# Attention beside a gated MLP: x written in twelve pieces, a second half that begins with the heads at hand, and PSUM banks in a fixed round

## The chip, the cores and the metric

The kernel runs on one core of a Trainium2 chip. The core's engines work side by side, each on its own queue of instructions in the order in which they are written: TensorE (PE, matmuls into the eight banks of PSUM), VectorE (DVE), ScalarE (ACT), GpSimd (POOL) and SyncE (SP), which issues nearly all DMAs here. The metric is the device time of one execution in microseconds (us), the median of several runs.

## The reference

```python
def _A_ref(x, k_cache, v_cache, wq, wo):        # 32 heads of 128, last W = 512 keys
    q = split_heads(x @ wq)
    k, v = k_cache[:, :, Sk - W:, :], v_cache[:, :, Sk - W:, :]
    scores = jnp.einsum("bhqd,bhkd->bhqk", q, k) * (Dh ** -0.5)
    p = _softmax(scores, axis=-1)
    o = jnp.einsum("bhqk,bhkd->bhqd", p, v)
    return merge_heads(o) @ wo

def _B_ref(x, w_in, w_sp, b_sp, w_out):          # F = 1376, Fh = 688
    z = _gelu(x @ w_in)
    z1, z2 = z[..., :Fh], _layernorm(z[..., Fh:], axis=-1)
    g = jnp.einsum("ts,bsf->btf", w_sp, z2) + b_sp[None, :, None]
    return (z1 * g) @ w_out

xn = _layernorm(x)                               # x is 2048 x 512, fp32
return x + _A_ref(xn, ...) * _silu(_B_ref(xn, ...))
```

(`split_heads` and `merge_heads` stand for the reshapes and transposes of the original.)

## The kernel before

All matrices are fp32. Each operand is split into a high part, cast to fp32r (`*_h`), and the rest (`*_l`), and a product is three matmuls: high by high, high by low, low by high (`mm3`, L65 to L67). ACT casts the high part, POOL or DVE subtracts to get the rest (`rest`, L59).

The attention makes up the first 1460 us. Its 2048 query rows are taken in two halves of 1024 (w = 0 and w = 1), each half for all 32 heads, and each head has two blocks of 512 rows per half: 128 blocks `b` in all, four steps of 128 rows each, 512 steps `t`, some 2.5 us per step while nothing waits. A head's weights (keys `("h", h), 1`, values `2`, output weights `3`) are loaded piece by piece into `raw` (256 KB, L102), cast (L141) and kept in `wt`; `plan` sets the step of the split and, six steps earlier, that of the load. The counter h runs to 64, and h modulo 32 is the head. Both halves take the heads in the order 0 to 31.

One step of the main loop issues, on PE in this order: the score of step t (`score`, into a bank `ps`), some products of the projection for later blocks (`q_products`, L447), the product of the shares with the values for step t - 13 (`pv`), and the out-product of step t - 18 (`outp`, into a bank `ps`). DVE takes the score's maximum (`nm`, L474), ACT the exponential (`prob`, L476, it reads `ps`), DVE adds the out-product to the sum (`sacc`, L533, it reads `ps`) and transposes the shares of the step before in blocks of 32 (L485, into `pL`). To finish the transposition, the four steps of a block are written together to memory (`p_dram<-pL`, 1 MB, L489) and come back in six loads (`pL<-p_dram`, L497, two steps later), ACT casts them at step t + 11 (`pT_h`, L504), POOL makes the rest (`pT_l`, L59), and `pv` reads both two steps after. What is put into the list `late` is issued on DVE at the end of the step; what is in `ends` is issued after that.

SP's queue holds all these transfers in the order of the steps: the raw loads at the start of a step, stores and loads of the shares at its end, and then what `ends` has. An SP DMA also waits until the eighth before it has landed. x, normalised and transposed, is held in the blocks `X[w]`. In the first half X[0] is written to memory for the end of the kernel (`keep_x`, four writes of 1 MB: one at step -2, three at steps 22, 25 and 28), and the rows of the second half are prepared (`later_x`: eight times four transposing matmuls, `flip`, L199, then row operations in `late`: L301, or `row_sums`, L234 to L236), and written to memory. X[1] is fetched back in 28 pieces (`fetch_part`, L263) at steps 232 to 246.

Of the eight PSUM banks four belong to `ps_acc` (projection and shares by values, `ps_a`), four to `ps_step`, one pool of four buffers of one name from which score, out-product, flip and some other products draw: it gives the bank that was released first.

```python
    ps_step = psum.enter_context(tc.tile_pool(name="ps_step", bufs=4, space=PSUM))
        ps = ps_step.tile([P, W], F32, name="ps_3")
```

After step 512 come the rest of the MLP's products, the spatial product and the output projection, which the change doesn't touch.

Of the kernel before, what the change touches and what calls it, by code (L numbers as in the profile page):

```python
# [8 lines left out]
F32 = mybir.dt.float32  # L9
# [31 lines left out]
def mixer_kernel(ctx: ExitStack, tc: tile.TileContext, x, wh, w_in, w_sp, b_sp, w_out, out):  # L41
# [8 lines left out]
    nc = tc.nc  # L50
# [7 lines left out]
    def rest(engine, lo, whole, hi):  # L58
        engine.tensor_tensor(lo, whole, hi.bitcast(F32), op=OP.subtract)  # L59
# [3 lines left out]
    def mm3(ps, first, last, lhs, rhs):  # L63
        (lh, ll), (rh, rl) = lhs, rhs
        nc.tensor.matmul(ps, lh, rh, start=first, stop=False)  # L65
        nc.tensor.matmul(ps, lh, rl, start=False, stop=False)  # L66
        nc.tensor.matmul(ps, ll, rh, start=False, stop=last)  # L67

    def cols(pair, lo, hi):
        return tuple(t[:, lo:hi] for t in pair)  # L70
# [10 lines left out]
    rawp = left.enter_context(tc.tile_pool(name="rawp", bufs=4))  # L81
    psum = ExitStack()
    ps_acc = psum.enter_context(tc.tile_pool(name="ps_acc", bufs=4, space=PSUM))
    ps_step = psum.enter_context(tc.tile_pool(name="ps_step", bufs=4, space=PSUM))
    att = ExitStack()
    sp = att.enter_context(tc.tile_pool(name="sp", bufs=1))
    ap = att.enter_context(tc.tile_pool(name="ap", bufs=2))
# [8 lines left out]

    raw, wt = {}, {}

    def load_piece(key, k):
        n = NB if key[0] == "w" else 512  # L100
        r = raw[key, k] = (xq.tile([P, 512], F32, name="rawx") if key[0] == "w" else rawp.tile([P, 512], F32, name="raw"))
        nc.sync.dma_start(r[:, :n], (w_in if key[0] == "w" else wh)[key[1] % H, :, k])  # L102

    def load_early(n, cs):
        if (n, "raw") not in raw:
# [44 lines left out]
    X = {0: {}, 1: {}}  # L150

    def block():
        return x8([P, 2, 2, 512])

    def quarter(t, j):
        return t[:, :, j * P:(j + 1) * P]
# [37 lines left out]
                nc.vector.tensor_scalar(sl, sl, mean, r, op0=OP.subtract, op1=OP.mult)  # L194

    def flip(t):
        ps = ps_step.tile([P, NC, P], F32, name="ps_3")
        for c in range(NC):
            nc.tensor.transpose(ps[:, c, :], t[:, c * P:(c + 1) * P], ident)  # L199
        return ps  # L200

    def ln_flip(i, parts=1):
        n, j = divmod(i, 4)
        if j == 0:
            for h in range(2):
                X[0][h, n] = block()
        if parts == 1:
            ps = flip(sacc[:, i, :])
        else:
            ps = ps_step.tile([P, NC, P], F32, name="ps_3")  # L210
        rests, rest_of = [], []
        for h in range(2):
            if parts > 1:
                for c in (2 * h, 2 * h + 1):
                    nc.tensor.transpose(ps[:, c, :], sacc[:, i, c * P:(c + 1) * P], ident)
            hi, lo = (quarter(X[0][h, n][:, a], j) for a in range(2))
            nc.scalar.copy(hi, ps[:, 2 * h:2 * h + 2])
            rests.append((lo, ps[:, 2 * h:2 * h + 2], hi))
        if n == 1:
            p2, y = ps.rearrange("p c q -> p (c q)"), sacc[:, i, :]  # L220
            nc.scalar.copy(y[:, :256], p2[:, :256])
            rest_of.append((y[:, 256:], p2[:, 256:], y[:, :256]))
# [20 lines left out]
    def t_split(p):  # L243
        y, o = sacc[:, 4 + p, :], sacc[:, p, :]
        for name, src in (("T2", o[:, 256:]), ("T1", o[:, :256]), ("T3", y[:, 256:]), ("T4", y[:, :256])):
# [4 lines left out]
    xd = {(w, k): dram.tile([P, 2, 2, 512], F32, name=f"x_dram{w}{n}")  # L250
          for w in range(2) for n, k in enumerate([(0, 0), (1, 0), (0, 1), (1, 1)] + list(TS) * w)}

    def keep_x(k):
        nc.sync.dma_start(xd[0, k], X[0][k].bitcast(F32))

    def fetch_x(w, k):
        X[w][k] = block()
# [77 lines left out]
    def zmm(ps, i, n, cs):  # L335
        for c in cs:
            mm3(ps, c == 0, c == NC - 1, tuple(x_op(i, a, c) for a in range(2)), cols(wt[("w", n), c], 0, NB))
# [8 lines left out]
                             start=k == 0, stop=k == len(order) - 1)  # L346

    def z1_product(i, n, between=lambda: None):
        ps = ps_acc.tile([P, 512], F32, name="ps_a") if n else ps_step.tile([P, 512], F32, name="ps_3")
        zmm(ps[:, :NB], i, n, range(2))  # L350
        between()
        zmm(ps[:, :NB], i, n, range(2, NC))
        return ps
# [49 lines left out]

    def load_q(g):
        r = wraw[g] = wq.tile([P, 2, 512], F32, name="wq", bufs=2)
        h = 2 * g % H
        for k in range(2):
            nc.sync.dma_start(r[:, k], wh[h + k, :, 0])

    def q_parts(g):  # L410
        r = wraw[g]
# [54 lines left out]

    def score(t):
        b, j = divmod(t, 4)
        ps = ps_step.tile([P, W], F32, name="ps_3")
        mm3(ps, True, True, cols(qT[b], j * P, (j + 1) * P), wt[("h", where(b)[0]), 1])  # L470
        if j == 0:
            sums[b] = ap.tile([P, 4], F32, name="sums", bufs=8)
        nm = ap.tile([P, 1], F32, name="nm", bufs=8)
        nc.vector.tensor_reduce(nm, ps, axis=AX.X, op=OP.max, negate=True)  # L474
        prob[t] = ap.tile([P, W], F32, name="prob", bufs=3)
        nc.scalar.activation(prob[t], ps, AF.Exp, bias=nm, accum_out=sums[b][:, j:j + 1])  # L476
# [46 lines left out]
    def outp(b, j):  # L523
        h, qb = where(b)
        i = qb * 4 + j
        at = sacc[:, i % T8, :]
        ps = ps_step.tile([P, D], F32, name="ps_3")
        mm3(ps, True, True, cols(oT[b], j * P, (j + 1) * P), wt[("h", h), 3])
        rs = sums[b][:, j:j + 1]
        if h % H == 0:  # L530
            nc.vector.tensor_scalar(at, ps, rs, None, op0=OP.mult)
        else:
            nc.vector.scalar_tensor_tensor(at, ps, rs, at, op0=OP.mult, op1=OP.add)  # L533
        if h % H == H - 1:
            nc.sync.dma_start(s_dram[:, i, :], at)
# [6 lines left out]
    def at(t, f, *args):  # L542
        todo.setdefault(t, []).append((f, args))
# [6 lines left out]

    for h in range(2 * H):
        for k, d in ((1, -4 if h else -5), (2, 6), (3, 11)):
            if h:
                plan(("h", h), k, 8 * h + d)
            elif k > 1:
                plan(("h", 0), k, d)
# [29 lines left out]
        at(-3 + p, t_sums, p)  # L586
        at(-2 + p, t_split, p)
    ends = {}
    for t, k in ((-2, (0, 1)), (22, (0, 0)), (25, (1, 0)), (28, (1, 1))):
        ends.setdefault(t, []).append((keep_x, k))  # L590
    for k, d in enumerate((4, 6, 8, 11, 13, 15, 17)):
        for n in range(4):
            ends.setdefault(16 * (NG // 2 - 1) - LEAD + d + (0, 0, 1, 1)[n], []).append((fetch_part, 1, ORDER[k], n))
# [26 lines left out]
    power = const.tile([P, 12], F32, name="power")  # L620
    nc.vector.memset(power, -0.5)

    warm = ps_step.tile([P, NC, P], F32, name="ps_3")
    for k in range(21):
        nc.tensor.transpose(warm[:, k % NC, :], ident, ident)
    bsp = const.tile([P, NT], F32, name="bsp")
# [13 lines left out]
        rest(nc.vector, *r)  # L640
    split_piece(w0, 2, nc.vector, True)
    split_piece(w0, 3, nc.vector, True)
    ps = ps_step.tile([P, 512], F32, name="ps_3")
    zmm_in(FIRST, ps[:, :NB], 0, 0)
    ln_flip(1)
    z1_out(0, 0, ps)
# [3 lines left out]
    for k in range(2, 4):  # L650
        split_piece(w1, k, nc.vector, True)
    ln_open(3)
    ps = ps_step.tile([P, 512], F32, name="ps_3")
    zmm_in(PAIRED, ps[:, :NB], 1, 0)
    z1_out(1, 0, ps)
    ln_apply(rows[2], 2)
# [1 line left out]
    ps = ps_acc.tile([P, 512], F32, name="ps_a")  # L658
# [18 lines left out]
    for t in range(T0, T1):  # L677
# [16 lines left out]
        if 0 <= t < NSTEP:  # L694
            score(t)
# [6 lines left out]
        g, s = divmod(t + LEAD, 16)  # L702
# [6 lines left out]
        if t in DRAIN:  # L709
            ps = z1_product(*DRAIN[t])  # L710
# [19 lines left out]
    ps = z1_product(*LAST[-1])  # L730
# [276 lines left out]
```

## Time and profile before

| | before |
|---|---|
| median of 3 runs (us) | 1825.79 (1825.51 to 1826.38) |
| the profiled execution (us) | 1828.83 |
| its span (us) | 1827.1 |
| PE busy (us, share) | 1799.5 (98%) |
| DVE, ACT, POOL busy | 76%, 64%, 68% |
| PE's longest waits in the attention | for ACT's pT_h 8.1 us (2 times), for DVE's sacc 4.3 us (7), for POOL's pT_l 4.1 us (8) |

A row of the timeline gives the start in us from the beginning of the span, the duration in us, engine, line, operation, the tile written and the tiles read, the shape and how many instructions the row joins; in brackets stands how long the engine was idle ahead of it and whose end released it. `SPq` rows are the issue of DMAs by SP; the landing is later. A row of stretches gives from:to and the length, then busy us and the count of records for PE, its weight loads, DVE, ACT and POOL, then the granted TensorE clock (1.00 is full), the share of time in which the DMA engines were busy, and GB/s. Matmuls overlap, so the distance of starts, and not the duration, is their cost.

### The profile page before, as it was taken

The numbers are of one execution on the slowest core, as the hardware profiler recorded it, in microseconds if no ns is written. First come the engines' busy times: TensorE is split into PE (matmuls) and PEld (weight loads), VectorE is DVE, ScalarE is ACT, GpSimd is POOL, SyncE is SP. The second block draws the span as 40 slices with busy tenths as digits, with TensorE's granted clock in tenths as the row PEclk, the third lists the DMA queues.
The fourth block names the chain that finished last, engine by engine and source line by source line (L and its number), as shares of the span: only waits on it lengthen the run. The fifth ranks groups of instructions, "written<-read, shape, count | busy, mean of one in ns | idle before, by whom it ended". The sixth has DMA issues, their size and how long they took to land.

```text
span 1827.1 us, 28750 instructions
## 1 busy us (share of the span) xinstructions
PE 1799.5 (98%) x8658; PEld 1540.9 (84%) x8658; DVE 1395.8 (76%) x2369; ACT 1175.7 (64%) x2631; POOL 1244.6 (68%) x1185
## 2 busy tenths in 40 slices
PE   8999999999999999999999999999999999999999
PEld 7787887888888887788888888888887999999998
DVE  5687988888898987788888888888888555333433
ACT  4676777777777775777777777777776444333422
POOL 3787898898898987888888888888887343000000
PEclk9999999999999999999999999999999999999999
DMA  5588787887887889888777777777778624554532
GB/s 184 175 278 239 236 256 219 255 248 224 248 243 240 252 243 291 243 265 246 227 225 223 220 223 227 224 231 229 217 223 253 218 91 155 176 179 141 184 119 92
DMA packets 181372, 395.65 MB, mean 217 GB/s; under 512 B 24320, under 2 KB 54784, under 8 KB 163680
## 3 DMA queue, kind: packets, MB, share of 16 engines
q1 hardware_dynamic: 176608, 388.17, 70.1%
q10 hardware_dynamic: 4608, 5.64, 0.9%
q8 instruction: 68, 1.11, 0.3%
q14 instruction: 88, 0.72, 0.1%
HBM read 226.99 MB, written 166.72 MB: 215 GB/s over the span
## 4 chain that ended last, share of the span: by engine, by line
PE 91%; DMA 5%; DVE 1%; POOL 1%; ACT 1%; issue 1%; SPq 0%; ACTq 0%; POOLq 0%; DVEq 0%
PE ps_a L447 15%; PE ps L65 12%; PE ps L67 12%; PE ps L66 12%; PE ps_a L66 8%; PE ps_a L67 8%; PE ps_a L65 8%; PE ps_g L66 4%; PE ps_g L65 4%; PE ps_g L67 4%; DMA p_dram<-pL 2%; DMA pL<-p_dram 1%; PE ps_f L65 1%; PE ps_f L66 1%; PE ps_f L67 1%; DMA raw<-wh 1%
## 5 line engine op out<-in xcount | busy, mean ns | idle before, releaser
L59 POOL TENSOR_TENSOR pT_l<-pL,pT_h 128x512 fp32r<-128x512 f32 x507 | 657.7, 1301 | 193.8 <-ACT pT_h L504 174.5
L476 ACT ACTIVATE prob<-ps,nm 128x512 f32<-128x512 f32 x512 | 353.9, 691 | 327.8 <-DVE nm L474 318.5
L533 DVE SCALAR_TENSOR_TENSOR sacc<-ps,sums,sacc 128x512 f32<-128x512 f32 x496 | 369.8, 746 | 126.2 <-PE ps L67 120.5
L447 PE MATMUL ps_a<-x,x 128*128 128x512 f32 x1302 | 376.6, 390 | 0.0
L485 DVE STREAM_TRANSPOSE pL<-prob 128x512 f32<-128x512 f32 x512 | 358.9, 701 | 16.2 <-ACT prob L476 16.2
L504 ACT CAST pT_h<-pL 128x512 fp32r<-128x512 f32 x512 | 318.3, 622 | 46.0 <-DMA pL<-p_dram 13.0
L474 DVE TENSOR_REDUCE nm<-ps 128x1 f32<-128x512 f32 x512 | 340.3, 665 | 7.1 <-PE ps L67 6.9
L447 PEld LDWEIGHTS ps_a<-x,x 128*128 128x128 f32 x1302 | 244.9, 188 | 51.4 <-PE ps L67 0.3
L59 POOL TENSOR_TENSOR wl<-raw,wh 128x512 fp32r<-128x512 f32 x192 | 249.7, 1300 | 11.1 <-ACT wh L141 11.1
L65 PE MATMUL ps_a<-pT_h,wh 128*128 128x512 f32 x512 | 200.5, 392 | 8.1 <-ACT pT_h L504 8.1
L66 PE MATMUL ps_a<-pT_l,wh 128*128 128x512 f32 x512 | 201.0, 393 | 4.3 <-POOL pT_l L59 4.1
L65 PE MATMUL ps<-wh,qT_h 128*128 128x512 f32 x512 | 201.2, 393 | 3.2 <-DVE sacc L533 3.2
L67 PE MATMUL ps<-wh,qT_l 128*128 128x512 f32 x512 | 200.3, 391 | 0.0
L66 PE MATMUL ps<-wl,qT_h 128*128 128x512 f32 x512 | 199.8, 390 | 0.0
L67 PE MATMUL ps<-wh,oT_l 128*128 128x512 f32 x512 | 199.8, 390 | 0.0
L67 PE MATMUL ps_a<-pT_h,wl 128*128 128x512 f32 x512 | 199.8, 390 | 0.0
L65 PE MATMUL ps<-wh,oT_h 128*128 128x512 f32 x512 | 199.8, 390 | 0.0
L66 PE MATMUL ps<-wl,oT_h 128*128 128x512 f32 x512 | 199.7, 390 | 0.0
L66 PE MATMUL ps_g<-z_l,x 128*128 128x344 f32 x512 | 162.1, 317 | 1.3 <-POOL z_l L59 1.3
L65 PE MATMUL ps_g<-z_h,x 128*128 128x344 f32 x512 | 162.1, 317 | 0.0
L67 PE MATMUL ps_g<-z_h,x 128*128 128x344 f32 x512 | 161.9, 316 | 0.0
L59 POOL TENSOR_TENSOR x<-wq,x 128x256 fp32r<-128x256 f32 x186 | 138.7, 746 | 1.5 <-ACT x L429 1.5
(203 smaller groups left out, 3186.0 us busy)
## 6 DMA issues: line engine op xcount, KB each, us to landing
p_dram<-pL SPq DMA_DIRECT2D x128, 1024.0 KB, 5.1
raw<-wh SPq DMA_DIRECT2D x194, 256.0 KB, 6.3
pL<-p_dram SPq DMA_DIRECT2D x256, 192.0 KB, 3.9
pL<-p_dram SPq DMA_DIRECT2D x256, 128.0 KB, 3.8
pL<-p_dram SPq DMA_DIRECT2D x256, 64.0 KB, 3.8
wq<-wh SPq DMA_DIRECT2D x62, 256.0 KB, 4.8
x<-w_sp SPq DMA_DIRECT2D x60, 256.0 KB, 6.0
x_dram<-rawx SPq DMA_DIRECT2D x32, 256.0 KB, 5.5
```

Of the source, the lines that this page charges most:

```text
L59: engine.tensor_tensor(lo, whole, hi.bitcast(F32), op=OP.subtract)
L65: nc.tensor.matmul(ps, lh, rh, start=first, stop=False)
L66: nc.tensor.matmul(ps, lh, rl, start=False, stop=False)
L67: nc.tensor.matmul(ps, ll, rh, start=False, stop=last)
L447: nc.tensor.matmul(qps[g, bank], wt["q", g, k][a][:, c * P:(c + 1) * P], X[g * 2 // H][ORDER[k]][:, b, c], start=first, stop=r == 5, skip_ ...
L474: nc.vector.tensor_reduce(nm, ps, axis=AX.X, op=OP.max, negate=True)
L476: nc.scalar.activation(prob[t], ps, AF.Exp, bias=nm, accum_out=sums[b][:, j:j + 1])
L485: nc.vector.transpose(pL[b][:, :, j * P:j * P + P].rearrange("p a (c q) -> p a c q", q=Q), prob.pop(t).rearrange("p (a c q) -> p a c q", a ...
L504: nc.scalar.copy(h, p)
L533: nc.vector.scalar_tensor_tensor(at, ps, rs, at, op0=OP.mult, op1=OP.add)
```

## The change

1. The three 1 MB writes of X[0] at steps 22, 25 and 28 become twelve writes of 256 KB, one every 16 steps from step 35 to step 211.
2. The second half takes the heads in the order 30, 31, 0, 1, ..., 29 (`head`). The weights of heads 30 and 31 are still in place from the end of the first half, so that their six loads, casts and rests at steps 246 to 275 are left out.
3. `ps_step` becomes four tiles of one buffer each, and a counter gives them out in a fixed round (`step_bank`): each request takes the bank of the fourth request before it.

```diff
-    ps_step = psum.enter_context(tc.tile_pool(name="ps_step", bufs=4, space=PSUM))
+    ps_step = psum.enter_context(tc.tile_pool(name="ps_step", bufs=1, space=PSUM))
+    banks = [0]
+
+    def step_bank(shape):
+        banks[0] += 1
+        return ps_step.tile(shape, F32, name=f"ps_{banks[0] % 4}")
...
+    def head(h):
+        return (h + (H - 2) * (h // H)) % H
...
-        nc.sync.dma_start(r[:, :n], (w_in if key[0] == "w" else wh)[key[1] % H, :, k])
+        nc.sync.dma_start(r[:, :n], w_in[key[1], :, k] if key[0] == "w" else wh[head(key[1]), :, k])
...
     def flip(t):
-        ps = ps_step.tile([P, NC, P], F32, name="ps_3")
+        ps = step_bank([P, NC, P])
...
-    def keep_x(k):
-        nc.sync.dma_start(xd[0, k], X[0][k].bitcast(F32))
+    def keep_x(k, *n):
+        to, of = (t[:, n[0] // 2, n[0] % 2] if n else t for t in (xd[0, k], X[0][k]))
+        nc.sync.dma_start(to, of.bitcast(F32))
...
     def load_q(g):
         r = wraw[g] = wq.tile([P, 2, 512], F32, name="wq", bufs=2)
-        h = 2 * g % H
         for k in range(2):
-            nc.sync.dma_start(r[:, k], wh[h + k, :, 0])
+            nc.sync.dma_start(r[:, k], wh[head(2 * g + k), :, 0])
...
     def score(t):
         b, j = divmod(t, 4)
-        ps = ps_step.tile([P, W], F32, name="ps_3")
+        ps = step_bank([P, W])
...
         at = sacc[:, i % T8, :]
-        ps = ps_step.tile([P, D], F32, name="ps_3")
+        ps = step_bank([P, D])
...
         for k, d in ((1, -4 if h else -5), (2, 6), (3, 11)):
-            if h:
+            if h in (H, H + 1):
+                at(8 * h + d, lambda h=h, k=k: wt.update({(("h", h), k): wt[("h", h - 2), k]}))
+            elif h:
                 plan(("h", h), k, 8 * h + d)
...
-    for t, k in ((-2, (0, 1)), (22, (0, 0)), (25, (1, 0)), (28, (1, 1))):
-        ends.setdefault(t, []).append((keep_x, k))
+    ends.setdefault(-2, []).append((keep_x, (0, 1)))
+    for n in range(12):
+        ends.setdefault(35 + 16 * n, []).append((keep_x, ((0, 0), (1, 0), (1, 1))[n // 4], n % 4))
```

The other places that drew from `ps_step` (`ln_flip`, `z1_product`, three products at the start) call `step_bank` in the same way.

SP's queue at the first 1 MB writes, before (`x_dram_98` and `x_dram_99` are the written copies of two blocks of X[0]):

```order
L497 DMA pL<-p_dram 32x3x512
L254 DMA x_dram_98<-x_180 128x2048
L102 DMA raw<-wh 128x512
L408 DMA wq<-wh 128x512 x2
L489 DMA p_dram<-pL 128x2048
L254 DMA x_dram_99<-x_181 128x2048
L497 DMA pL<-p_dram 32x3x512
```

The same place after the change:

```order
L506 DMA pL<-p_dram 32x3x512
L111 DMA raw<-wh 128x512
L417 DMA wq<-wh 128x512 x2
L498 DMA p_dram<-pL 128x2048
L506 DMA pL<-p_dram 32x3x512
```

The first piece, some blocks later, after the change:

```order
L506 DMA pL<-p_dram 32x2x512 x2
L506 DMA pL<-p_dram 32x512
L506 DMA pL<-p_dram 32x3x512
L264 DMA x_dram_98<-x_180 128x512
L498 DMA p_dram<-pL 128x2048
L111 DMA raw<-wh 128x512 x2
```

The writes are gone from between the stores and loads of two blocks in a row; a piece comes after the last load of a block and ahead of the store of the next.

SP's queue near the end of the fetches for the second half, before (`x_8862` and `x_8936` are blocks of X[1]; the two raw loads are the output weights of head 30 and the first piece for h = 32):

```order
L489 DMA p_dram<-pL 128x2048
L263 DMA x_8862<-x_dram_105 128x512 x2
L102 DMA raw<-wh 128x512
L263 DMA x_8936<-x_dram_109 128x512 x2
L102 DMA raw<-wh 128x512
L497 DMA pL<-p_dram 32x3x512
```

After the change:

```order
L498 DMA p_dram<-pL 128x2048
L273 DMA x_8871<-x_dram_105 128x512 x2
L111 DMA raw<-wh 128x512
L273 DMA x_8945<-x_dram_109 128x512 x2
L506 DMA pL<-p_dram 32x3x512
```

One raw load is left out ahead of the six loads of the shares; the fetches and the store keep their places.

PE at a flip of the first half (the fourth of the eight), from the flip of step t to the out-product of step t + 1, with the waits in brackets, before (`ps_` and a number is one request of a bank of the round; `qT_h` stands in a score, `oT_h` in an out-product):

```order
L199 MATMUL ps_4098<-ident,rawx 128x128 [waits DVE_49]
L199 MATMUL ps_4098<-ident,rawx 128x128 x3
L65 MATMUL ps_4107<-wh_3922,qT_h 128x512 [waits DVE_49]
...
L65 MATMUL ps_4121<-wh_3616,oT_h 128x512 [waits Activation_49]
...
L65 MATMUL ps_4143<-wh_3922,qT_h 128x512 [waits Activation_49]
...
L65 MATMUL ps_4157<-wh_3892,oT_h 128x512 [waits DVE_49,Activation_49]
```

After the change:

```order
L208 MATMUL ps_4100<-ident,rawx 128x128 [waits Activation_49]
L208 MATMUL ps_4100<-ident,rawx 128x128 x3
L65 MATMUL ps_4109<-wh_3924,qT_h 128x512 [waits DVE_49]
...
L65 MATMUL ps_4123<-wh_3617,oT_h 128x512 [waits Activation_49]
...
L65 MATMUL ps_4145<-wh_3924,qT_h 128x512 [waits DVE_49]
...
L65 MATMUL ps_4159<-wh_3893,oT_h 128x512 [waits DVE_49,PE_49,Activation_49]
```

The order of PE's work is the same in both; the flip waits for ACT where it had waited for DVE, and the next step's score for DVE where it had waited for ACT.

PE at step 253, the first that needs the block that comes late in the second stall of the prediction, before:

```order
L65 MATMUL ps_9180<-wh_8869,qT_h 128x512 [waits DVE_49]
L66 MATMUL ps_9180<-wl_8870,qT_h 128x512
L67 MATMUL ps_9180<-wh_8869,qT_l 128x512
L447 MATMUL ps_a<-x_8720,x_751 128x512
L447 MATMUL ps_a<-x_8792,x_751 128x512 [waits DMAHW1_49,Activation_49]
L447 MATMUL ps_a<-x_8792,x_751 128x512 [waits DMAHW1_49]
L65 MATMUL ps_a<-pT_h,wh_8945 128x512 [waits Activation_49]
L66 MATMUL ps_a<-pT_l,wh_8945 128x512 [waits Pool_49]
```

After the change:

```order
L65 MATMUL ps_9183<-wh_8878,qT_h 128x512 [waits Activation_49]
L66 MATMUL ps_9183<-wl_8879,qT_h 128x512
L67 MATMUL ps_9183<-wh_8878,qT_l 128x512
L456 MATMUL ps_a<-x_8729,x_751 128x512
L456 MATMUL ps_a<-x_8801,x_751 128x512 [waits DMAHW2_49] x2
L65 MATMUL ps_a<-pT_h,wh_8952 128x512
L66 MATMUL ps_a<-pT_l,wh_8952 128x512 [waits Pool_49]
```

The wait for ACT has moved from the product with the shares (`pT_h`) to the score ahead of it, and what it waits for there is an exponential that stands behind the cast of `pT_h` on ACT.

More of the change, by code (lines that the diff above doesn't have):

```diff
@@ L209, in ln_flip @@
         else:
-            ps = ps_step.tile([P, NC, P], F32, name="ps_3")
+            ps = step_bank([P, NC, P])
         rests, rest_of = [], []
@@ L348, in z1_product @@
     def z1_product(i, n, between=lambda: None):
-        ps = ps_acc.tile([P, 512], F32, name="ps_a") if n else ps_step.tile([P, 512], F32, name="ps_3")
+        ps = ps_acc.tile([P, 512], F32, name="ps_a") if n else step_bank([P, 512])
         zmm(ps[:, :NB], i, n, range(2))
@@ L621, in mixer_kernel @@
     nc.vector.memset(power, -0.5)
-    warm = ps_step.tile([P, NC, P], F32, name="ps_3")
+    warm = step_bank([P, NC, P])
     for k in range(21):
@@ L642, in mixer_kernel @@
     split_piece(w0, 3, nc.vector, True)
-    ps = ps_step.tile([P, 512], F32, name="ps_3")
+    ps = step_bank([P, 512])
     zmm_in(FIRST, ps[:, :NB], 0, 0)
@@ L652, in mixer_kernel @@
     ln_open(3)
-    ps = ps_step.tile([P, 512], F32, name="ps_3")
+    ps = step_bank([P, 512])
     zmm_in(PAIRED, ps[:, :NB], 1, 0)
```

## The prediction

> **What bounds the kernel now.** I read the page first, then the stretches of 40 us, then the rows of the two stretches that fall short, and last the waits for PSUM. Page and stretches (us from the start; matmul records in brackets; then the granted clock, the DMA share and GB/s):
>
> ```profile
> span 1827.1 us, 28750 instructions
> PE 1799.5 (98%) x8658; PEld 1540.9 (84%) x8658; DVE 1395.8 (76%) x2369; ACT 1175.7 (64%) x2631; POOL 1244.6 (68%) x1185
> ...
> 120.00:160.00 40.00, 35.64 (x144) 28.12 (x143) 28.26 (x48) 22.70 (x53) 29.90 (x28) 0.91 0.86 256
> 480.00:520.00 40.00, 40.00 (x178) 33.14 (x177) 35.77 (x60) 30.29 (x71) 37.68 (x37) 1.00 0.88 270
> 720.00:760.00 40.00, 35.12 (x141) 27.53 (x140) 27.59 (x47) 23.04 (x55) 26.89 (x26) 0.91 0.77 225
> ```
>
> TensorE (PE) is the bound, and an undisturbed stretch holds 178 matmuls, 0.225 us each. Two stretches fall short: 34 matmuls (7.7 us) and 37 (8.3 us). Everything else that the change touches is worth an us or less at a time, so these two stalls and the new waits decide.
>
> The first stall, by the rows of SP's queue, ACT and PE, and the clock in stretches of 1 us and after:
>
> ```profile
> 110.14 0.41 SPq L254 DMA_DIRECT2D x_dram<-x  x1
> ...
> 114.04 0.48 SPq L254 DMA_DIRECT2D x_dram<-x  x1
> 121.31 2.66 SPq L497 DMA_DIRECT2D pL<-p_dram  x6
> 124.01 0.43 SPq L489 DMA_DIRECT2D p_dram<-pL  x1
> 124.49 0.43 SPq L254 DMA_DIRECT2D x_dram<-x  x1
> ...
> 130.10 7.92 SPq L497 DMA_DIRECT2D pL<-p_dram  x6
> ...
> 143.69 0.62 ACT L504 CAST pT_h<-pL 128x512 fp32r<-128x512 f32 x1 [7.60 <-DMA pL<-p_dram]
> ...
> 139.72 0.84 PE L447 MATMUL ps_a<-x,x 128*128 128x512 f32 x3
> 144.36 0.79 PE L65 MATMUL ps_a<-pT_h,wh 128*128 128x512 f32 x1 [3.80 <-ACT pT_h L504]
> ...
> 143.00:144.00 1.00, 0.00 (x0) 0.00 (x0) 0.00 (x0) 0.31 (x1) 0.00 (x0) 0.87 0.88 369
> 144.00:145.00 1.00, 0.64 (x1) 0.29 (x1) 0.00 (x0) 1.00 (x3) 0.62 (x1) 0.50 0.54 229
> ...
> 144.30:150.50 6.20, 5.58 (x12) 4.10 (x13) 3.25 (x6) 5.30 (x14) 6.12 (x6) 0.50 0.46 144
> ```
>
> Three 1 MB writes of x surround a store of a block's shares. The six loads behind the store take 7.92 us to issue instead of 2.66. ACT, free from 136.09 (143.69 - 7.60), waits for them; PE idles from 140.56; its clock falls 3.3 us later and stays at half for some 6 us.
>
> **The writes in twelve pieces.** Without the big writes, I let the store issued at 124.01 land after the page's median and the loads go out at the undisturbed rate:
>
> ```profile
> p_dram<-pL SPq DMA_DIRECT2D x128, 1024.0 KB, 5.1
> ...
> pL<-p_dram SPq DMA_DIRECT2D x256, 128.0 KB, 3.8
> ...
> L504 ACT CAST pT_h<-pL 128x512 fp32r<-128x512 f32 x512 | 318.3, 622 | 46.0 <-DMA pL<-p_dram 13.0
> ...
> 160.00:640.00 480.00, 477.17 (x2110) 392.24 (x2109) 431.54 (x741) 361.15 (x850) 424.20 (x410) 1.00 0.81 243
> ```
>
> 124.01 + 5.1 + 2.66 + 3.8 = 135.6, before ACT is free at 136.1, and far before PE runs dry. The stall goes: -7.7. Each piece of 256 KB takes 256 / 243 = 1.1 us of all the DMA engines (by the GB/s of the last row), is queued behind a block's six loads and ahead of the next store, and holds SP until one of its slots is free. The cover is what the loads land ahead of their cast: 2.0 to 6.1 us for the twelve blocks concerned, by the rows of the queue and of ACT. ACT waited for these loads 13.0 us in the whole run, 7.60 of it in the first stall and none of it between 160 and 640 us, at a DMA share of 0.81. I take 0; the bounds are -0.2 (nothing there to gain) and, if each piece cost half its 1.1 us, +6.
>
> **The fixed round of banks.** Before, the bank released first is taken; now each request gets the bank of the fourth request before it. That takes away these waits and makes others:
>
> ```profile
> PE ps L65 <- DVE sacc L533: 4.3, 7, 1.1
> ...
> 180.80 0.60 PE L199 MATMUL ps<-ident,rawx 128*128 128x128 f32 x4
> 186.05 0.39 PE L65 MATMUL ps<-wh,oT_h 128*128 128x512 f32 x1
> 186.14 0.41 DVE L301 TENSOR_TENSOR rawx<-ps,rawx 128x256 f32<-128x256 f32 x1
> ...
> 585.54 0.75 DVE L533 SCALAR_TENSOR_TENSOR sacc<-ps,sums,sacc 128x512 f32<-128x512 f32 x1 [1.23 <-PE ps L67]
> 587.38 0.39 PE L65 MATMUL ps<-wh,oT_h 128*128 128x512 f32 x1
> 588.25 0.42 DVE L236 TENSOR_TENSOR rawx<-ps,rawx 128x256 f32<-128x256 f32 x1
> ...
> 329.97 0.50 PE L65 MATMUL ps<-wh,qT_h 128*128 128x512 f32 x1 [0.41 <-DVE sacc L533]
> ```
>
> Eight times in the first half rows of x are flipped (L199). The round then runs flip, score, out-product of step t, score, out-product of step t+1: the last gets the flip's bank, and must wait until VectorE has finished the flip's row operations, which `late` puts at the end of step t. At the first flip that end is 186.55 and the product wants to start at 186.05; at the last 588.67 against 587.38, although VectorE was idle for 1.23 us before the chain. The eight lacks are 0.50, 1.36, 1.10, 1.29, -0.37, 1.00, 1.10 and 1.29, in order of time. A restart costs some 0.16 (a matmul after a wait has 0.50 instead of 0.39, and 0.05 from release to start). Where PE waited ahead of this chain in before (0.41 + 0.11 at 329.97, alike at the third flip), that wait goes and the chain comes earlier by it; the fifth has its -0.37 behind a wait of 0.95 that goes. Net: 0.66 + 1.51 + 0.70 + 0.89 - 0.21 + 1.16 + 1.26 + 1.45 = +7.4. One wait for sacc stands apart from the flips: -0.4. Queued behind the waiting product are only PE's own next steps. Bounds: 0, if VectorE got its row operations done in time, and +9, with no credit for the old waits.
>
> A score now waits for the exponential of two steps before. At the start this bites once:
>
> ```profile
> 96.38 0.39 PE L65 MATMUL ps<-wh,qT_h 128*128 128x512 f32 x1
> ...
> 96.26 0.68 ACT L476 ACTIVATE prob<-ps,nm 128x512 f32<-128x512 f32 x1
> ```
>
> 96.94 - 96.38 + 0.16 = +0.7. In the drain (1389 to 1413 us) four scores and products come within 0.02 us of such an end: +0.3.
>
> **The second half's beginning.** Six raw loads, six casts and six rests go. The rows around the second stall:
>
> ```profile
> 712.80 0.32 SPq L489 DMA_DIRECT2D p_dram<-pL  x1
> ...
> 715.49 1.20 SPq L102 DMA_DIRECT2D raw<-wh  x1
> ...
> 717.82 0.42 SPq L102 DMA_DIRECT2D raw<-wh  x1
> 721.75 4.82 SPq L497 DMA_DIRECT2D pL<-p_dram  x6
> ...
> 725.78 0.39 PE L65 MATMUL ps<-wh,qT_h 128*128 128x512 f32 x1
> ...
> 731.60 0.80 PE L65 MATMUL ps_a<-pT_h,wh 128*128 128x512 f32 x1 [4.30 <-ACT pT_h L504]
> ...
> 730.93 0.62 ACT L504 CAST pT_h<-pL 128x512 fp32r<-128x512 f32 x1 [7.76 <-DMA raw<-wh]
> ...
> 732.28 0.68 ACT L476 ACTIVATE prob<-ps,nm 128x512 f32<-128x512 f32 x1
> ```
>
> What is late is the store of 712.80 and the six loads behind it, among 28 fetches of x. Of the six dropped loads only that of 717.82 stands ahead of them; the others come after the stall, under a PE that does not wait. Without it the sixth load of the block no longer needs its slot and goes out some 1.3 us earlier; I let the data land at 729.2 instead of about 730.9. But the score at 725.78 will now wait for the exponential that ends at 732.96 in before: 2.03 us after the landing, since three other instructions of ACT stand between. So PE stops at 725.9 and restarts at 731.2: 5.3 us idle, the clock falls again, and at 731.2 six matmuls (a score and its projections) are still to do that before had behind it. Half clock for 5.9 us gives some 14 matmuls by 737.1, 15 by 737.4, when before has 6 + 12: three late, +0.7. Bounds: -5.0 (8.3 less 3.3), if the data land by 727.2, so that PE restarts within the 3.3 us after which the clock fell; +2.4, if they land no earlier. The dropped casts and rests are worth nothing: ACT and POOL wait there for the data.
>
> The Trainium skill ("TensorE: Matmul & The Clock Gate", Part 1: The HAM clock gate) says that the clock is full again after about 3.4 us of sustained work. Here it was at half for 5.9 to 6.2 us after either stall (731.6 to 737.4 the second time). By the page's figure the changed kernel would do 3.4 / 0.43 + 2.8 / 0.225 = 20 matmuls by 737.4 instead of 15, and the term would be -0.5 (an estimate); the sum goes by the rows.
>
> **The sum.** -7.7 + 7.4 - 0.4 + 0.7 + 0.3 + 0.7 = +1.0. The profiled run took 1828.83 (span 1827.1, 1.7 around it), 3.0 above the median of 1825.79; on the median the forecast is 1826.8. Changes under 0.2% (3.65 us) count as no change: this kernel's three runs lie within 0.9 us, but two kernels cannot be told apart much better. So: no measurable change, the stall of the first half traded for the waits at the flips.
>
> **Rivals.**
> Faster (a): the data of the second half land by 727.2. For it: one write less in a crowded stretch. Against: five of six loads come too late, and the store of 712.80 is untouched. 1826.8 - 0.7 - 5.0 = 1821.1. Chance 0.12.
> Faster (b): the waits at the flips do not bite, because VectorE, relieved where PE pauses, is earlier than its rows of before. Against: the lack of 1.29 stands at a flip where it had been idle for 1.23. 1826.8 - 7.4 = 1819.4. Chance 0.08.
> Slower (c): the pieces cost. It decides where a block's slack is under 1.1 us; there are blocks of 0.5 us of slack, but none behind a piece. 1826.8 + 6 = 1833. Chance 0.10.
> Slower (d): the change does not remove the first stall, because the fetches of x and of weights at the same place make it. Against: the loads' issue alone grew by 5.3 us between two big writes. 1826.8 + 7.7 = 1834.5. Chance 0.06.
> Slower (e): the short waits make the clock fall. In before it did not: the row below has a wait of 0.84 twice and clock 1.00. If six of the eight did, at 6 us of half clock each, +18: 1845. Chance 0.03.
>
> ```profile
> 440.00:480.00 40.00, 39.16 (x175) 32.05 (x174) 35.11 (x61) 30.12 (x71) 31.30 (x30) 1.00 0.73 223
> ```
>
> The Trainium skill (same page, "A second HAM failure mode: psum-queue depth-cycling") tells of a kernel whose PE idled a little at every round of its PSUM banks, and whose clock swung for it; by that rule (e) would be what happens. The trace speaks against it.
>
> **How the numbers follow.** The forecast keeps 0.61, of which its own errors (some 2 us for the flips, 2 for the second half) push 0.02 below and 0.04 above the bound. Faster 0.12 + 0.08 + 0.02 = 0.22, slower 0.10 + 0.06 + 0.03 + 0.04 = 0.23, the same 0.55. The range goes from (b) to (c): 1819 to 1833; the forecast's own is 1823 to 1830.
>
> **What would show it.** 120 to 160 us at 176 matmuls or more and clock 1.00; after each of the flips but one a wait of 0.5 to 1.4 us of an out-product for VectorE's L301 or L236 of before; no wait for sacc ahead of a score; at about 726 us PE stopping ahead of a score, for the exponential, with the clock at half behind it; loads undisturbed between 160 and 640 us. The forecast falls if that second stall is short, if the flips do not wait, or if ACT waits for a block behind a piece.

## The result, and the profile after

| | before | after |
|---|---|---|
| median (us), 22 runs of each | 1827.55 (1824.95 to 1831.17) | 1831.64 (1827.73 to 1836.61) |
| ratio to before, 95% interval | | 1.0021 (1.0014 to 1.0029) |
| span of the profiled execution (us) | 1827.1 | 1829.9 |
| TensorE clock, mean over the span | 0.995 | 0.996 |

The change makes the kernel slower by 0.21%, some 3.9 us. That lies in the range of 1819 to 1833 and on the edge of what the prediction called no change (0.2%); the interval reaches to both sides of that edge, so that the likeliest case was missed by very little, on the slower side. The runs also showed that the kernel's times lie 6 to 9 us apart from run to run, more than the three runs shown before the prediction told; why is said at the end.

The page of after, and the stretches that answer to those of before:

```profile
span 1829.9 us, 28781 instructions
PE 1795.9 (98%) x8658; PEld 1539.5 (84%) x8658; DVE 1396.6 (76%) x2369; ACT 1172.6 (64%) x2625; POOL 1237.0 (68%) x1179
...
80.00:120.00 40.00, 36.85 (x152) 29.29 (x152) 29.71 (x50) 27.81 (x66) 33.40 (x32) 0.96 0.79 234
120.00:160.00 40.00, 40.00 (x179) 33.11 (x177) 35.70 (x62) 28.60 (x68) 34.57 (x33) 1.00 0.84 242
160.00:640.00 480.00, 469.52 (x2068) 385.44 (x2067) 423.23 (x726) 353.34 (x831) 418.38 (x405) 1.00 0.81 244
680.00:720.00 40.00, 38.59 (x170) 31.33 (x169) 33.49 (x56) 27.79 (x67) 32.95 (x31) 1.00 1.02 294
720.00:760.00 40.00, 34.48 (x139) 27.93 (x140) 28.34 (x47) 23.08 (x55) 26.46 (x26) 0.91 0.81 254
```

The first stall is gone (179 matmuls at full clock from 120 to 160 us, where before had 144), the second is there (139, before 141). The long stretch between lost 42 matmuls against before's 2110, some 9.5 us, and 80 to 120 us lost 13 against this row of before:

```profile
80.00:120.00 40.00, 38.23 (x165) 30.36 (x165) 32.57 (x56) 30.20 (x72) 36.54 (x36) 1.00 0.84 262
```

Which waits these are, by the view of PE's waits and the timeline's rows of PE (the line numbers of after are 9 to 10 higher: L485 is the exponential, L245 and L311 the last row operations on a flip; in the runs below they differ again by a few):

```profile
PE ps L65 <- ACT prob L485: 10.7, 6, 5.5
PE ps L65 <- DVE rawx L245: 6.5, 4, 2.2
PE ps L65 <- DVE rawx L311: 3.4, 4, 1.1
...
96.64 0.63 PE L65 MATMUL ps<-wh,qT_h 128*128 128x512 f32 x1 [2.21 <-ACT prob L485]
180.80 0.47 PE L65 MATMUL ps<-wh,oT_h 128*128 128x512 f32 x1 [0.48 <-DVE rawx L311]
204.32 0.47 PE L65 MATMUL ps<-wh,oT_h 128*128 128x512 f32 x1 [1.66 <-DVE rawx L245]
287.40 0.50 PE L65 MATMUL ps<-wh,qT_h 128*128 128x512 f32 x1 [0.55 <-ACT prob L485]
309.74 0.47 PE L65 MATMUL ps<-wh,oT_h 128*128 128x512 f32 x1 [1.09 <-DVE rawx L311]
333.01 0.47 PE L65 MATMUL ps<-wh,oT_h 128*128 128x512 f32 x1 [1.40 <-DVE rawx L245]
437.25 0.47 PE L65 MATMUL ps<-wh,oT_h 128*128 128x512 f32 x1 [0.77 <-DVE rawx L311]
461.26 0.47 PE L65 MATMUL ps<-wh,oT_h 128*128 128x512 f32 x1 [2.16 <-DVE rawx L245]
567.63 0.47 PE L65 MATMUL ps<-wh,oT_h 128*128 128x512 f32 x1 [1.09 <-DVE rawx L311]
590.77 0.47 PE L65 MATMUL ps<-wh,oT_h 128*128 128x512 f32 x1 [1.28 <-DVE rawx L245]
708.95 0.50 PE L65 MATMUL ps<-wh,qT_h 128*128 128x512 f32 x1 [1.41 <-ACT prob L485]
736.14 0.79 PE L65 MATMUL ps<-wh,qT_h 128*128 128x512 f32 x1 [5.52 <-ACT prob L485]
```

All eight flips make their out-product wait, for 0.48 to 2.16 us (0.5 to 1.4 us, at all but one, was expected). Scores wait for the exponential at 96.64 and 736.14 us, as expected, and also at 287.40 and 708.95 us, which was not. At the first of these two places the score of before had waited for VectorE's sum, a wait that was to go:

```profile
290.55 0.50 PE L65 MATMUL ps<-wh,qT_h 128*128 128x512 f32 x1 [0.33 <-DVE sacc L533]
```

PE's order of work is the same in both kernels, and the trace has the start of each of the 512 scores in both. How far after lies behind before at a score, and what each stage adds to it, gives the account of the profiled executions:

| stage (steps) | predicted (us) | after against before (us) |
|---|---|---|
| up to the first score | 0 | -1.29 |
| start (to step 36) | +0.7 | +3.05 |
| first stall (to step 46) | -7.7 | -7.65 |
| flips (to step 244) | +7.0 | +9.32 |
| second stall (to step 264) | +0.7 | +1.28 |
| drain (to step 511) | +0.3 | -1.40 |
| sum | +1.0 | +3.31 |

### The profile page after: what moved, and what is told of

Its sections match the earlier page's. It is cut to its first block, busy times and chain, and to the rows that moved or that the text cites. A ratio compares the mean times of both kernels' runs of the same rounds, so it can differ in the third digit from the quotient of the medians.

```text
span 1829.9 us, 28781 instructions
## 1 busy us (share of the span) xinstructions
PE 1795.9 (98%) x8658; PEld 1539.5 (84%) x8658; DVE 1396.6 (76%) x2369; ACT 1172.6 (64%) x2625; POOL 1237.0 (68%) x1179
## 4 chain that ended last, share of the span: by engine, by line
PE 91%; DMA 4%; DVE 3%; ACT 1%; issue 1%; POOL 1%; SPq 0%; ACTq 0%; DVEq 0%; POOLq 0%
PE ps_a L456 15%; PE ps L65 12%; PE ps L67 12%; PE ps L66 12%; PE ps_a L66 8%; PE ps_a L65 8%; PE ps_a L67 8%; PE ps_g L66 4%; PE ps_g L67 4%; PE ps_g L65 4%; DMA pL<-p_dram 2%; DMA p_dram<-pL 1%; PE ps_f L67 1%; PE ps_f L66 1%; PE ps_f L65 1%
## 5 line engine op out<-in xcount | busy, mean ns | idle before, releaser
L485 ACT ACTIVATE prob<-ps,nm 128x512 f32<-128x512 f32 x512 | 353.6, 691 | 356.0 <-DVE nm L483 346.2
L59 POOL TENSOR_TENSOR wl<-raw,wh 128x512 fp32r<-128x512 f32 x186 | 241.3, 1297 | 11.1 <-ACT wh L150 11.1
```

## The experiments

All ratios are to the kernel before, run beside it on the same chip, with a 95% interval.

**Each part alone.** First the pieces: the kernel before with `keep_x` and its schedule from the change, nothing else.

```diff
-    for t, k in ((-2, (0, 1)), (22, (0, 0)), (25, (1, 0)), (28, (1, 1))):
-        ends.setdefault(t, []).append((keep_x, k))
+    ends.setdefault(-2, []).append((keep_x, (0, 1)))
+    for n in range(12):
+        ends.setdefault(35 + 16 * n, []).append((keep_x, ((0, 0), (1, 0), (1, 1))[n // 4], n % 4))
```

> The kernel before with the twelve pieces alone. Theory (the first stall is made by the three 1 MB writes, the pieces are hidden): 7.7 us less than before, 6 to 9, a ratio of 0.995 to 0.997; 120 to 160 us at 176 matmuls or more and clock 1.00; the second stall as in before. Rival (the pieces cost where they now stand, between 160 and 640 us): 0 to 4 us less, and ACT or PE waiting for loads of the shares in that stretch.

Measured: 1822.6 against 1827.86, ratio 0.9975 (0.9966 to 0.9984), some 4.6 us less. The profile shows the first stall gone and no cost from 160 to 640 us, where before has 2110 matmuls:

```profile
120.00:160.00 40.00, 40.00 (x178) 33.12 (x177) 35.79 (x62) 28.88 (x68) 34.53 (x33) 1.00 0.85 247
160.00:640.00 480.00, 477.16 (x2111) 392.41 (x2110) 430.35 (x738) 361.32 (x851) 427.13 (x413) 1.00 0.82 249
...
720.00:760.00 40.00, 35.99 (x145) 29.17 (x146) 29.14 (x50) 27.41 (x64) 33.27 (x32) 0.91 0.79 240
```

In this profile the stage of the first stall gained 7.76 us, in the timed runs the whole gain was 4.6, less than the 6 to 9 expected. The cause was real and the size open; three more profiles were taken for it, below.

Then the heads: the kernel before with `head`, the reused entries of `wt` and the loads by `head`.

> The kernel before with the second half's order of heads alone. Theory (five of the six loads come after the stall; the one ahead lets the data land 1 to 1.5 us earlier): 1 to 3 us less, 0.998 to 0.9995, PE still waiting at about 727 us for pT_h, 2.5 to 3.5 us instead of 4.3, the first stall as in before. Rival (the loads left out end the second stall): 7 us less or more, 720 to 760 us at 170 matmuls or more.

Measured: 1827.29, ratio 0.9994 (0.9983 to 1.0004): not told from before. The first stall is as it was, the second shorter:

```profile
146.70 0.80 PE L65 MATMUL ps_a<-pT_h,wh 128*128 128x512 f32 x1 [3.79 <-ACT pT_h L510]
...
732.09 0.50 PE L65 MATMUL ps_a<-pT_h,wh 128*128 128x512 f32 x1 [2.08 <-ACT pT_h L510]
```

PE waits 2.08 us for the block instead of 4.30, as the data come about 2 us earlier, counted from PE's steps; the stage of the second stall gained 3.1 us in this profile.

Then the round: the kernel before with `step_bank`.

> The kernel before with the fixed round of banks alone. Theory (the round costs what the profile after shows at the flips, some 9 to 10 us, and 1 to 4 us at the start and in the second half): 9 to 14 us more than before, 1.005 to 1.008, both stalls there, each seen as a wait of a score for the exponential. Rival (the round itself is neutral, what was seen at the flips is waiting that only changed its place): 0 to 3 us more.

Measured: 1836.84, ratio 1.0055 (1.0042 to 1.0069), some 10 us more.

```profile
PE ps L65 <- ACT prob L484: 16.4, 8, 7.3
PE ps L65 <- DVE rawx L245: 6.2, 4, 2.2
PE ps L65 <- DVE rawx L310: 3.4, 4, 1.1
...
144.64 0.79 PE L65 MATMUL ps<-wh,qT_h 128*128 128x512 f32 x1 [5.61 <-ACT prob L484]
742.64 0.80 PE L65 MATMUL ps<-wh,qT_h 128*128 128x512 f32 x1 [7.35 <-ACT prob L484]
```

The round is not neutral. The same eight waits as in after stand at the flips; that stage costs 7.38 us here. Both stalls begin a score earlier, since the score waits for the exponential: 5.61 us idle where before has 3.80, 7.35 where it has 4.30. In the account of the stages this costs +0.6 at the first stall and +2.4 at the second.

**The change without the round.** Pieces and heads, with `ps_step` as in before:

```diff
-    ps_step = psum.enter_context(tc.tile_pool(name="ps_step", bufs=1, space=PSUM))
+    ps_step = psum.enter_context(tc.tile_pool(name="ps_step", bufs=4, space=PSUM))
...
-        banks[0] += 1
-        return ps_step.tile(shape, F32, name=f"ps_{banks[0] % 4}")
+        return ps_step.tile(shape, F32, name="ps_3")
```

> The changed kernel with the pool of four buffers that gives the bank released first (pieces and heads, no round). Theory: the two gains stand alone, 8 to 11 us less than before, 0.994 to 0.9955, and 12 to 15 us less than the changed kernel; no out-product waits for a flip's row operations. Rival (the round is neutral): 3 to 5 us more than before, like the changed kernel.

Measured: 1822.56, ratio 0.9972 (0.9963 to 0.9981): 5.1 us less than before and 9 less than the change, where 8 to 11 and 12 to 15 were expected. So the round's price of 9 to 10 us is there in both surroundings, with and without the other two parts, and the parts add up: -4.6 - 1 + 10 = +4. No out-product waits for a flip, and PE waits 2.66 us instead of 5.52 in the second stall:

```profile
728.05 0.74 PE L65 MATMUL ps_a<-pT_h,wh 128*128 128x512 f32 x1 [2.66 <-ACT pT_h L511]
```

**Is it the flip's bank?** The changed kernel, with one bank left out of the round after each flip, so that the next step's out-product gets the bank of the score ahead.

```diff
-    banks = [0]
+    banks = [0, 99]
 
     def step_bank(shape):
         banks[0] += 1
+        banks[1] += 1
+        if banks[1] == 4:
+            banks[0] += 1
...
             ps = flip(t[i]).rearrange("p c q -> p (c q)")
+            banks[1] = 0
```

> The changed kernel, but after a flip the round leaves out one bank, so that the out-product of the next step takes the bank of the score before instead of the flip's. Theory (the round's price is the eight waits for VectorE's row operations, 9.9 us in the profile after, and one fall of the clock behind the longest): 7 to 10 us less than the changed kernel, 1822 to 1825, a ratio to before of 0.997 to 0.9985; no out-product waits for row operations; the waits of scores for the exponential stay. Rival (VectorE is simply late at these places, whatever bank is asked for): the waits move to another product or score, 0 to 3 us less.

Measured: 1825.09, ratio 0.9983 (0.9974 to 0.9993), 6.5 us less than the change's median; the expected 7 to 10 was missed by little.

```profile
PE ps L65 <- ACT prob L489: 12.8, 11, 4.4
...
160.00:640.00 480.00, 477.12 (x2107) 391.24 (x2106) 430.58 (x740) 360.57 (x849) 426.52 (x412) 1.00 0.83 248
...
332.65 0.50 PE L65 MATMUL ps<-wh,oT_h 128*128 128x512 f32 x1 [0.66 <-ACT prob L489]
459.49 0.50 PE L65 MATMUL ps<-wh,oT_h 128*128 128x512 f32 x1 [1.42 <-ACT prob L489]
728.63 0.79 PE L65 MATMUL ps<-wh,qT_h 128*128 128x512 f32 x1 [4.43 <-ACT prob L489]
```

No product waits for row operations any more, and 160 to 640 us has 2107 matmuls again (before 2110, the change 2068). Three of the eight waits came back smaller (0.66, 1.42 and 0.16 us), for an exponential. VectorE is as late as it was: its row operations end 5.75 to 7.20 us after the flip, at each of the eight within 0.01 us of the round alone. What made PE wait was that this one bank was asked for. What is left against the pool (2.5 us by the medians, 2.0 by the ratios) is not settled by the two profiles, whose runs took 1824.70 and 1824.48 us. The rows to suspect are the eleven waits for an exponential, 12.8 us with the second stall's.

**Is it the crowd of fetches?** The 28 fetches for the second half spread over steps 232 to 254, in the changed kernel and in the one without the round.

```diff
-    for k, d in enumerate((4, 6, 8, 11, 13, 15, 17)):
+    for k, d in enumerate((4, 7, 11, 14, 18, 21, 24)):
         for n in range(4):
-            ends.setdefault(16 * (NG // 2 - 1) - LEAD + d + (0, 0, 1, 1)[n], []).append((fetch_part, 1, ORDER[k], n))
+            ends.setdefault(16 * (NG // 2 - 1) - LEAD + d + (0, 1, 1, 2)[n], []).append((fetch_part, 1, ORDER[k], n))
```

> The changed kernel with the 28 fetches for the second half spread over steps 232 to 254 instead of 232 to 246 (the same fetches, in the same order). Theory (the fetches crowd the queue and make the second stall): 6 to 9 us less than the changed kernel, 1822 to 1826; 720 to 760 us at 172 matmuls or more and clock 1.00. Rival (the stall comes from the round, a score waiting for the exponential): less than 2 us.

> Pieces and heads with the pool that gives the bank released first, and the 28 fetches spread over steps 232 to 254. Theory: 5 to 8 us less than pieces and heads without the spreading, 1814 to 1818, a ratio to before of 0.993 to 0.995, both stalls gone, and runs that lie closer together, since what is left varies less. Rival (the spread fetches come too late for the projections that read them): a new wait of PE for a DMA between 740 and 790 us, no gain.

Measured: 1829.68, ratio 1.0012 (1.0002 to 1.0021), with the round; 1820.94, ratio 0.9961 (0.9946 to 0.9975), without. Some 2 us or less each against the same kernel with the fetches close together, where 6 to 9 and 5 to 8 were expected. But the theory did not fall with it. The waits at 709 and 736 us of the change and the one at 728 us of the kernel without the round are gone; in their place stands, in the spread kernel with the round and then in the one without:

```profile
741.93 1.55 PE L456 MATMUL ps_a<-x,x 128*128 128x512 f32 x3 [3.63 <-DMA x<-x_dram]
```

```profile
735.14 1.65 PE L454 MATMUL ps_a<-x,x 128*128 128x512 f32 x3 [4.96 <-DMA x<-x_dram]
```

The rival written for the second of them happened: thinned so far, a fetch comes too late for its projection. Spread over steps 232 to 248 only, without the round:

```diff
-    for k, d in enumerate((4, 6, 8, 11, 13, 15, 17)):
+    for k, d in enumerate((4, 7, 9, 12, 15, 17, 19)):
```

> Pieces and heads, the pool that gives the bank released first, and the 28 fetches spread over steps 232 to 248 only (between before's 246 and the 254 that was too late for the projections). Theory: the crowd thins enough that PE idles less than 2 us at about 727 us and the fetches still land before their projections: 3 to 7 us less than pieces and heads alone, 1815 to 1820, 0.993 to 0.9955. Rival (the crowd cannot be thinned without a late fetch): PE waits 2 us or more, for the shares or for a fetch, and the time is that of pieces and heads, 1822 to 1823.

Measured: 1821.29 (1820.09 to 1821.88) against 1827.85, ratio 0.9961 (0.9946 to 0.9975): 6.6 us less than before and 10 less than the change, a little above the expected 1815 to 1820.

```profile
720.00:760.00 40.00, 36.89 (x157) 28.66 (x156) 30.54 (x51) 25.72 (x61) 29.70 (x28) 1.00 0.79 261
...
724.94 0.49 PE L65 MATMUL ps_a<-pT_h,wh 128*128 128x512 f32 x1 [0.99 <-ACT pT_h L511]
```

PE waits 0.99 us for the block, the clock stays full, and that stage is 4.4 us shorter than in before. With the crowd of fetches thinned, in these three kernels, no wait for the shares of 1 us or more is left there: the crowd makes the second stall. The gain over pieces and heads alone (1822.56) is no more than these runs can tell, and in this profile the stage of the flips was 2.5 us longer than in before, in waits up to 206 us that weren't followed up.

**Which idle time costs the clock.** The changed kernel with 4 to 9 extra reductions on VectorE at the end of every twelfth step from 282 on, whose results nothing reads, so that PE waits for different times.

```diff
+        if t in range(282, 500, 12):
+            n = DOSES[(t - 282) // 12 % len(DOSES)]
+            for k in range(n):
+                dose = ap.tile([P, 1], F32, name="dose", bufs=2)
+                late.append((nc.vector.tensor_reduce, dose, sacc[:, k % T8, :], AX.X, OP.max))
```

> The changed kernel with 4 to 9 extra reductions on VectorE, of some 0.6 us each, at the end of every twelfth step from 282 to 498, so that PE waits once per site for 0.5 to 4 us. It measures which idle time makes the clock fall. Theory (by the two falls in the profile after, behind waits of 2.2 us, and none behind 1.7): the clock falls behind waits from about 2 us on, depending on where the wait lies, and stays at half for 3.4 us or 6.8. Rival (what I took from the two stalls before): it falls only behind waits of 3.3 us or more.

One run, 1886.96 us. Three of its waits, and the clock in the 3.5 us behind the first two:

```profile
930.80 0.50 PE L65 MATMUL ps<-wh,qT_h 128*128 128x512 f32 x1 [2.21 <-ACT prob L485]
1000.85 0.50 PE L65 MATMUL ps<-wh,qT_h 128*128 128x512 f32 x1 [2.80 <-ACT prob L485]
1377.74 0.50 PE L65 MATMUL ps<-wh,qT_h 128*128 128x512 f32 x1 [1.82 <-ACT prob L485]
...
931.00:934.50 3.50, 3.50 (x10) 2.73 (x10) 2.93 (x7) 2.33 (x6) 2.67 (x3) 0.54 0.07 25
1001.00:1004.50 3.50, 3.50 (x16) 2.87 (x17) 3.50 (x8) 2.39 (x6) 2.79 (x3) 1.00 0.35 116
```

The wait of 2.21 us cost the clock, the longer one did not, and behind the third, of 1.82 us, the clock fell at 1378.46 us. The theory was right that waits of about 2 us can do it, and the rival (3.3 us) is refuted; what decides is told at the end.

**What varies in the pieces.** The pieces alone, profiled twice more, and the kernel before once more.

> The kernel before with the twelve pieces alone, a second profile. Theory (its gain in the timed runs, 4.6 us, was less than in its first profile because what is left varies by run: the second stall and the clock behind it, the waits near the start): the first stall is gone again, 120 to 160 us at 176 matmuls or more; what differs from the first profile lies at 80 to 110 us and at 700 to 745 us. Rival (the pieces cost something between 160 and 640 us in most runs): waits of PE for the shares in that stretch.

> The same, a third profile, with the same expectations of both.

> The kernel before, a second profile. Theory: both stalls again, 141 to 148 matmuls in 120 to 160 us and in 720 to 760 us; the first within 1 us of its first profile, the second less alike. Rival (the first stall is not in every run): 170 matmuls or more in 120 to 160 us.

Measured: 1826.65, 1821.37 and 1828.86. The stages against before's first profile:

| stage | pieces, 1st | 2nd | 3rd | before, 2nd |
|---|---|---|---|---|
| up to the first score | +0.59 | +2.24 | +0.54 | +0.76 |
| start | -1.01 | +0.67 | -0.99 | -0.18 |
| first stall | -7.76 | -6.03 | -6.53 | -0.38 |
| flips | -0.17 | +0.28 | -0.01 | -0.18 |
| second stall | -0.06 | +2.00 | -0.44 | +0.58 |
| drain | -0.46 | -1.43 | -0.40 | -0.58 |
| sum | -8.87 | -2.27 | -7.83 | +0.02 |

The first stall is in each profile of a kernel with the 1 MB writes and in none with the pieces, but the stage gains 6.0 to 7.8 us, not always 7.7; the stretch of the pieces is the same to 0.3 us in all. The rival (a cost there) is out. The rest differs by how late the first score comes, at the start and around the second stall. The second profile in the stretch of the first stall, with PE's waits there, and the third:

```profile
120.00:160.00 40.00, 38.83 (x171) 31.48 (x170) 33.53 (x57) 27.17 (x64) 33.37 (x32) 1.00 0.77 222
...
143.80 0.50 PE L66 MATMUL ps_a<-pT_l,wh 128*128 128x512 f32 x1 [0.40 <-POOL pT_l L59]
146.94 0.47 PE L448 MATMUL ps_a<-x,x 128*128 128x512 f32 x1 [0.78 <-DVE oT_l L59]
```

```profile
120.00:160.00 40.00, 39.21 (x173) 31.90 (x172) 34.51 (x60) 27.78 (x65) 33.08 (x32) 1.00 0.87 253
```

Against the theory's 176 or more, the second and the third profile have 171 and 173: small waits, for POOL and for VectorE, take a part of the gain back there. All ten profiles of kernels with the pieces give that stage -6.0 to -7.8 us, -6.8 on the mean. The timed gain of 4.6 us (2.9 to 6.2) is less, but the profiled runs are single runs: the three of the pieces took 1820.06, 1826.65 and 1821.37 us, 1822.7 on the mean, close to their timed median of 1822.6, while both of before (1828.83 and 1828.86) lay 1.0 us above its median of 1827.86. With that taken off, the profiles' gain is 5.2 us, inside the interval. What else lies between stage and whole, at the start and around the second stall, stays open.

## Why the prediction was right or wrong

**The range held; the likeliest case was missed by a hair.** 1831.64 lies in 1819 to 1833; the forecast of +1.0 us became +3.9 (2.6 to 5.3 by the interval), and the ratio 1.0021 is just beyond the bound for no change. The chances gave 0.55 to no change and 0.23 to slower. That the sum came so near is in part luck: in the profile after the start and the flips cost 4.7 us more than forecast, but 1.3 us of it only used up an earlier first score, and a drain shorter by 1.7 us than forecast made up for as much; neither was foreseen.

**The writes in pieces: mechanism right, size too large by some 1 to 3 us.** The profile after shows the full -7.65, but ten profiles with the pieces show -6.0 to -7.8, -6.8 on the mean, and the timed runs of the pieces alone -4.6. I had priced the gain as all that the stretch lost, at one profile, and had not counted the small waits that appear there when the stall is gone, for POOL (0.40) and VectorE (0.78) in the second profile of the pieces. "I take 0" for the pieces was right: 2111 matmuls against 2110 in the stretch where they stand. Rivals (c) and (d) did not happen.

**The flips: right in place and size, without the clock.** At the fifth and the sixth flip (-0.37 and 1.00) a wait of 0.84 us ahead of them goes, 0.95 with its restart, so that the waits to be seen are 0.58 and 1.95. With these two, the forecast of 0.50, 1.36, 1.10, 1.29, 0.58, 1.95, 1.10 and 1.29 was measured as 0.48, 1.66, 1.09, 1.40, 0.77, 2.16, 1.09 and 1.28. The list of signs overlooked this and gave 1.4 as the longest. With the round alone the stage cost 7.38 us against +7.0. The -0.4 in it did not come: the score that had waited 0.33 us for VectorE's sum waits 0.55 us for an exponential. In the profile after the stage cost 9.32, because the clock fell behind the wait of 2.16; that is the 1.7 us which rival (e) priced far too high (one wait of eight, and 3.4 us of half clock, not six at 6) and which the sum left out. My reason against (e), waits of 0.84 at full clock, reached no farther than 0.84. Rival (b) is refuted by the eight waits themselves: VectorE was no earlier.

**The start: undersized.** I took the one row where a score came 0.56 us before the exponential's end, +0.7. In the profile after PE came there 2.1 us earlier than in before, 1.3 by the earlier first score and 0.8 by a wait for POOL that before has at 87.44 us; the exponential ended only 0.45 us earlier (96.49 against 96.94). So PE waited 2.21 us and lost the clock: +3.05 for the stage, of which 1.3 is only the earlier beginning given back. In the four other kernels with the round the same score waited 0.50 (the round alone), 1.04, 1.44 and 1.81 us. The step that failed is the use of before's time at which PE arrives; the size hangs on it.

**The second half: right in the stall, with one wait missed.** +0.7 was predicted, +1.28 measured in the profile after: 5.52 us idle (5.3 predicted) ahead of the score, for the exponential, and half clock for 6.83 us, of which 5.8 (5.9 predicted) lie behind the wait. The wait of 1.41 us at 708.95 was in no term; it is there with the round alone too (1.25 us) and gone when the fetches are spread. The two parts of the working are shown apart by the single parts: the heads shorten PE's wait from 4.30 to 2.08 us, the round lengthens it by 3.1 without the heads and by 2.9 with them (2.66 to 5.52). My bound for rival (a), that a wait under 3.3 us keeps the clock, is refuted: 2.08 and 2.66 us cost it too. Only at 0.99 us was it kept.

**The drain** came out 1.4 us shorter, not 0.3 longer. The kernels with the round show -1.15 to -1.51 there (the one with added work aside), those without it -0.40 to -1.43, the pool and the second profile of the pieces as much as after: it is not shown to come from the change. The waits for the exponential that I priced at +0.3 are there (0.34 and 0.64 us), in the place of waits for VectorE's sum (0.35 and 1.09 us in before).

## What to carry to other kernels

A pool that hands out the buffer released first kept a slow reader of one buffer out of everybody's way here; a fixed round makes each request wait for one certain reader, and the one that read last set the price. Before such a round is put in, list for each request who read the buffer n requests ago and when that reader ends: this list, made from the rows of before, gave the eight waits here to 0.3 us, once the waits that go were counted in. And a stall that one transfer makes should be costed by what the other engines will do when it is gone, not by all that the stretch lost.

## What was not expected of the hardware

The clock does not fall after a certain idle time. In every profile the falls lie whole multiples of 3.413 us apart, and half clock lasts 3.41 or 6.83 us (unless the run ends), by the trace's record of the clock. I laid this grid over the 75 waits of PE of 0.9 us or more between the first score and the last in fourteen profiles and took for each the largest part of one grid interval that it filled. Of 46 that filled at most 0.50 of an interval none made the clock fall, one of 2.80 us among them; of 24 that filled 0.60 or more all did, the shortest with 2.16 us; of the five between, three did, with waits of 1.81, 1.82 and 2.08 us. (Ahead of the first score, where several short waits share an interval, the clock also fell where the longest of them filled as little as 0.23; these are not counted.) How long half clock lasts goes by the same grid: at the 11 of these 27 falls with 3.41 us, PE idled for at most 0.08 of the first interval behind the fall; at the 16 with 6.83 us, for 0.17 or more.

So a wait of 1.8 to 2.8 us costs the clock or not by where it lies on the grid. The wait of 2.16 us at the sixth flip made it fall in after, which cost 1.7 us; the same wait in the round alone and in the spread kernel did not. That is a part of the spread of 6 to 9 us between runs of one kernel: over the 22 runs of after the mean clock lay between 0.994 and 0.998, lower in the slower runs (correlation -0.73). The Trainium skill ("TensorE: Matmul & The Clock Gate", Part 1: The HAM clock gate) says that the window is about 3.4 us, runs freely and does not start with the kernel, which these runs bear out; it gives an idle window as the condition, and here little more than half a window of idling was enough.
